# A recurrent attention kernel, forward and backward: steps in three head parts, division after the weighted sum, output projections split by output columns

## The chip, the cores and the metric

The kernel runs on one core of one Trainium2 chip. The metric is the device time of one execution in microseconds (us). The profile used here is one execution taken by the hardware profiler. Its engines are PE (matrix multiplications), PEld (the loading of a matmul's stationary operand, the "weights", which may overlap PE), DVE, ACT and POOL (elementwise engines) and SP (which issues the DMA transfers). "Granted clock" is the share of PE's full clock that the profile says was granted.

## The reference

The reference computes a block with layer norm, a dense MLP with squared ReLU, and a recurrent attention, and then all gradients. Cut to what matters (S = 2048 rows, D = 512, 32 heads of 128, segments of 32 rows, 8 memory rows):

```python
mem = mem0
for s in range(64):
    xs = x[:, s*32:(s+1)*32, :]
    h = concatenate([mem, xs], axis=1)            # 8 + 32 = 40 rows
    q, k, v = h @ Wq, h @ Wk, h @ Wv              # per head
    p = softmax(where(mask, q @ k.T * scale, -1e9))
    o = (p @ v) @ Wo                              # sum over heads and their 128 columns
    mem = o[:, :8, :]                             # the next segment's memory
    outs.append(o[:, 8:, :])
out = x + concat(outs) + mlp(layernorm(x))        # xs are rows of layernorm(x)
# then jax.vjp(out): gradients of x, mem0, Wq, Wk, Wv, Wo, w1, b1, w2, b2
```

The memory makes both directions serial: 64 forward steps, then 64 backward steps in reverse order, each needing the result of the one before.

## The kernel before

The program has seven stretches: MLP and weight transposes; projections of the rows that no later step needs (the first 8 rows of each segment, the "left rows"); the forward recurrence; the left rows' attention; the backward recurrence; the left rows' gradients; and the weight gradients. The 32 heads are spread as 4 groups (g) of 8 (k). A step's 32 rows take 32 of the array's 128 columns, so four matmuls, one a group, stand side by side as column tiles (`tile_position=(0, 32 * g)`).

A projection over all heads is summed. Each of the four column tiles holds the partial sum of its own group; a matmul with a selection matrix adds the four:

```python
# forward, after the weighted sum:
def wo_half(R, OT, B):
    for k in range(B * KK, (B + 1) * KK):
        for g in range(HG):
            nc.tensor.matmul(R[32 * g:32 * g + 32, :], lhsT=OT[:, k, g, :], rhs=Wo[:, g * KH + k, :],
                             start=(k == 0), stop=(k == KH - 1), tile_position=(0, 32 * g))
# backward, three such sums (t = v, k, q) of 8 * 4 matmuls 512 columns wide:
def back_proj(gTs):
    R = pbig("ps_gR")
    ...
            nc.tensor.matmul(R[32 * g:32 * g + 32, :], lhsT=gX[:, k, g], rhs=WT[t][:, g * KH + k, :], ...)
    Rs = bs.tile([P, D], F32, name="bRs", tag="bRs")
    nc.any.tensor_copy(Rs[:], R[:])
# ... and the sum over groups, which gives the next step's input:
    for dc in range(DC):
        nc.tensor.matmul(psm[:, dc * M:(dc + 1) * M], lhsT=Rs[:, dc * P:(dc + 1) * P], rhs=sel[:],
                         start=True, stop=True)
```

At the end of each backward step, three gradient tiles are turned and written out, through a staging tile with two buffers:

```python
def spill_nat(gX, t, r0):
    gN = bs.tile([P, GW], BF16, name="gNat", tag="gNat")        # pool bs: two buffers
    for B in range(2):
        ps = trp.tile([P, 1024], BF16, name="ps_nat", tag="tr")
        for k in range(KK):
            transpose_to(ps[:, k * P:(k + 1) * P], gX[:, B * KK + k])
        nc.any.tensor_copy(gN[:, B * 512:(B + 1) * 512], ps[:, 0:512])
    dma(S_G[r0:r0 + 32, t, :].rearrange("r (g c) -> g r c", g=HG), gN[:])   # 256 KB, shape [4][32][1024]
```

The left rows' gradients and the sums over groups for the output rows come after the recurrence, block by block, for 16 blocks (`left_done`, `finish_back`, which calls `sum_rows` over four stored partial sums).

## Time and profile before

| | us |
|---|---|
| median of 4 runs | 5743.66 (5728.2 to 5751.35) |
| MLP, weight transposes | 712 |
| left-row projections | 152 |
| forward recurrence, 64 steps | 1321 |
| left-row attention, 16 blocks | 666 |
| backward recurrence, 64 steps | 1698 |
| left-row gradients, 16 blocks | 344 |
| weight gradients, with a gap | 852 |

The same kernel by stretches. The columns are the stretch, its length, the busy us and instructions of PE, PEld, DVE, ACT and POOL, then the granted clock, the DMA engines' share and GB/s. The five stretches shown are the forward recurrence, the left rows' attention, the backward recurrence, the left rows' gradients, and the gap in the weight gradients:

```profile
864.00:2185.00 1321.00, 1086.75 (x17016) 525.44 (x17008) 406.54 (x1155) 526.35 (x1022) 66.44 (x186) 0.83 0.33 107
2185.00:2851.00 666.00, 318.15 (x6046) 196.21 (x6046) 214.79 (x624) 223.22 (x704) 154.73 (x144) 0.59 0.52 169
2851.00:4549.00 1698.00, 1164.14 (x20900) 662.96 (x20904) 455.52 (x2045) 503.14 (x1277) 17.27 (x66) 0.75 0.38 111
4549.00:4893.00 344.00, 163.38 (x2009) 73.38 (x2000) 32.65 (x74) 39.05 (x67) 50.79 (x43) 0.71 0.40 125
...
5326.00:5602.00 276.00, 2.60 (x13) 1.06 (x12) 17.14 (x36) 0.58 (x1) 66.39 (x57) 0.51 0.24 73
```

In the last one PE did 2.6 us of work in 276: it waited for the chain of group sums.

One backward step in the chain of work that ended last (start us, us, what; the short pieces left out):

```profile
3508.60 7.58 PE ps_gR L677 x95
3516.20 0.59 ACT bRs L681
3516.84 1.07 PE ps_bm L894 x8
3518.22 0.40 PE ps_nat L201 x4
3518.64 0.43 DVE gNat L691
3519.13 7.75 DMA S_G<-gNat
3527.01 0.44 DVE gNat L691
...
3535.29 7.88 PE ps_gR L677 x94
```

A backward step of 26.5 us is thus about 7.8 us of waiting for a store (the third gNat needs the buffer of the first, whose 256 KB must have landed), about 8 us of flips, scores and outer products, about 8 us of the 512-wide sum `ps_gR`, and 1.7 us of group sum. The waits of that stretch say the same (waiter, what it waited for: us in total, times, longest):

```profile
DVE gNat L691 <- DMA S_G<-gNat: 420.8, 63, 6.9
...
PE ps_tr L201 <- DVE gNat L691: 322.5, 63, 5.4
```

### The profile page before, as it was taken

Reading aid. Unit: us, or ns where it says so; the run is one execution under the profiler, and the core shown is the slowest. Engines: PE = TensorE matmul, PEld = TensorE weight load, DVE = VectorE, ACT = ScalarE, POOL = GpSimd, SP = SyncE. Lnnn points to the kernel's source line nnn. Section 1 sums busy time; section 2 is a strip of 40 time slices with the busy share of each in tenths; the row PEclk is TensorE's granted clock in tenths of the full one; section 3 lists DMA queues with packets and bytes.
Section 4 is the critical chain, followed back from the end, with each engine's and each line's share of the span. In section 5 each row is a group of like instructions: output and inputs, shape, how many; then the busy total and the mean of one; then the engine's idle time right before and its main releaser. Section 6 shows DMA issues by size and latency. Waiting matters only on the chain.

```text
span 5745.4 us, 121908 instructions
## 1 busy us (share of the span) xinstructions
PE 3770.1 (66%) x52292; PEld 1932.4 (34%) x52292; DVE 1368.9 (24%) x4348; ACT 1525.5 (27%) x3440; POOL 440.7 (8%) x619
## 2 busy tenths in 40 slices
PE   3923588888888884555376666767667644899009
PEld 2511233343443432333233333333333322344004
DVE  5610023333333332333222222222222201000000
ACT  1300033444444442333222323222232211011001
POOL 0000000000000001222200000000000011111220
PEclk8966898888888886565577777777777777899559
DMA  5296553333333325455543433333333334666222
GB/s 167 111 210 185 192 204 105 105 104 107 107 104 107 105 96 202 158 155 168 172 118 107 118 108 112 113 111 114 107 113 111 91 119 138 221 211 227 87 59 103
DMA packets 517090, 768.84 MB, mean 134 GB/s; under 512 B 152882, under 2 KB 230339, under 8 KB 513987
## 3 DMA queue, kind: packets, MB, share of 16 engines
q1 hardware_dynamic: 516546, 761.04, 42.4%
q8 instruction: 409, 6.70, 0.5%
q14 instruction: 135, 1.10, 0.1%
HBM read 401.22 MB, written 343.42 MB: 130 GB/s over the span
## 4 chain that ended last, share of the span: by engine, by line
PE 49%; DMA 25%; DVE 11%; ACT 7%; SPq 4%; issue 3%; POOL 2%; DVEq 0%; POOLq 0%; ACTq 0%
PE ps_gR L677 9%; DMA S_G<-gNat 9%; PE ps_proj L423 7%; PE ps_gw L929 7%; PE ps_tr L201 6%; PE ps_R L524 4%; PE ps_out L666 3%; PE ps_gwo L942 2%; PE ps_m L620 2%; PE ps_wgh L474 1%; DMA gXL<-S_GL 1%; ACT OT L433 1%; DMA S_PART<-part 1%; PE ps_bm L894 1%; DMA S_WT<-wtt 1%
## 5 line engine op out<-in xcount | busy, mean ns | idle before, releaser
L423 PE MATMUL ps_proj<-Wqkv,hT 128*32 128x512 bf16 x6144 | 488.1, 423 | 0.3 <-DVE hT L572 0.3
L691 DVE COPY gNat<-ps_nat 128x512 bf16<-128x512 bf16 x239 | 101.4, 424 | 1422.0 <-PE ps_nat L201 870.1
L201 PE MATMUL ps_tr<-ident,gON 128*128 128x128 bf16 x640 | 88.6, 287 | 327.8 <-DVE gNat L691 322.5
L929 PEld LDWEIGHTS <-HNc 128*128 128x128 bf16 x1920 | 188.2, 98 | 265.2 <-issue 40.0
L691 ACT COPY gNat<-ps_nat 128x512 bf16<-128x512 bf16 x241 | 141.1, 585 | 496.4 <-DMA S_G<-gNat 431.8
L524 PE MATMUL ps_R<-Wo,OT 128*32 128x512 bf16 x2048 | 172.5, 469 | 86.2 <-ACT OT L433 86.2
L677 PE MATMUL ps_gR<-WT_28394,gv 128*32 128x512 bf16 x2048 | 224.0, 615 | 0.0
L942 PE MATMUL ps_gwo<-GOc,on_71965 128*128 128x512 bf16 x160 | 36.5, 392 | 273.4 <-DMA GOc<-S_GO 273.4
L681 ACT COPY bRs<-ps_gR 128x512 f32<-128x512 f32 x80 | 46.8, 585 | 622.3 <-PE ps_gR L677 614.2
L423 PEld LDWEIGHTS <-hT 128*32 128x32 bf16 x6144 | 151.5, 102 | 172.9 <-issue 72.7
L423 PE MATMUL ps_proj<-WoT,goT 128*32 128x512 bf16 x2048 | 159.8, 386 | 39.2 <-POOL goT L841 39.2
L201 PEld LDWEIGHTS <-gON 128*128 128x128 bf16 x640 | 55.1, 121 | 342.4 <-issue 321.1
L677 PE MATMUL ps_gR<-WT_28396,gk 128*32 128x512 bf16 x2048 | 166.5, 483 | 0.0
L666 PE MATMUL ps_out<-gST,b_kN 32*128 32x32 bf16 x2048 | 129.6, 184 | 30.0 <-DVE gkL L877 23.6
L433 DVE COPY vT<-ps_tr 128x512 bf16<-128x512 bf16 x65 | 27.6, 425 | 503.1 <-issue 481.7
L474 PEld LDWEIGHTS <-PT 32*32 32x32 bf16 (+1 forms) x5120 | 94.2, 105 | 147.1 <-DVE PT L465 89.4
L899 POOL COPY goT<-gTblk 128x96 bf16<-128x96 bf16 x63 | 16.8, 267 | 1606.3 <-PE ps_proj L423 1606.3
L382 PE MATMUL ps_w_2850<-ghn,xnN 128*128 128x512 bf16 x16 | 6.2, 389 | 191.7 <-DMA ghn<-S_GH1N 191.7
L620 PE MATMUL ps_m<-sel,Rs 128*128 128x8 f32 x504 | 100.2, 327 | 43.5 <-ACT Rs L613 43.5
L479 ACT CAST ON<-ps_wgh 128x512 bf16<-128x512 f32 x128 | 74.9, 585 | 193.6 <-PE ps_wgh L474 193.6
L666 PE MATMUL ps_out<-gST,b_kLs 8*128 8x32 bf16 x2048 | 124.6, 183 | 0.8
L620 PEld LDWEIGHTS ps_m<-sel,Rs 128*128 128x128 f32 x504 | 94.3, 280 | 84.5 <-ACT Rs L613 84.5
(944 smaller groups left out, 7256.4 us busy)
## 6 DMA issues: line engine op xcount, KB each, us to landing
S_G<-gNat SPq DMA_DIRECT2D x240, 256.0 KB
S_PART<-part SPq DMA_DIRECT2D x128, 256.0 KB
b_part<-S_PART SPq DMA_DIRECT2D x64, 512.0 KB
S_VTA<-vT SPq DMA_DIRECT2D x64, 320.0 KB
b_vT<-S_VTA SPq DMA_DIRECT2D x64, 320.0 KB
S_KA<-kN SPq DMA_DIRECT2D x64, 256.0 KB
S_QA<-qN SPq DMA_DIRECT2D x64, 256.0 KB
S_VA<-vN SPq DMA_DIRECT2D x64, 256.0 KB
```

Of the source, the lines that this page charges most:

```text
L201: nc.tensor.transpose(ps_ap, in_ap, ident[base:base + k, base:base + k])
L423: nc.tensor.matmul(ps[32 * g:32 * g + 32, :], lhsT=hT[:, dc, :], rhs=W[:, dc, c:c + 512], start=(dc == 0), stop=(dc == DC - 1), tile_posit ...
L433: nc.any.tensor_copy(dst, ps[:, 0:KK * P].rearrange("p (k g r) -> p k g r", k=KK, g=HG))
L474: nc.tensor.matmul(ps[32 * g:32 * g + 32, k * P:(k + 1) * P], lhsT=PT[32 * g:32 * g + n, k, i, :], rhs=V[32 * g:32 * g + n, (B * KK + k) * ...
L479: nc.any.tensor_copy(dst[:, B * 512:(B + 1) * 512], ps[:])
L524: nc.tensor.matmul(R[32 * g:32 * g + 32, :], lhsT=OT[:, k, g, :], rhs=Wo[:, g * KH + k, :], start=(k == 0), stop=(k == KH - 1), tile_posit ...
L620: nc.tensor.matmul(psm[:, dc * M:(dc + 1) * M], lhsT=Rs[:, dc * P:(dc + 1) * P], rhs=sel[:], start=True, stop=True)
L666: nc.tensor.matmul(p3[:, k, :], lhsT=N_[32 * g:32 * g + m, k * P:(k + 1) * P], rhs=X(k)[32 * g:32 * g + m], start=(i == 0), stop=(i == len ...
L677: nc.tensor.matmul(R[32 * g:32 * g + 32, :], lhsT=gX[:, k, g], rhs=WT[t][:, g * KH + k, :], start=(i == 0), stop=(i == 3 * KH - 1), tile_p ...
L691: nc.any.tensor_copy(gN[:, B * 512:(B + 1) * 512], ps[:, 0:512])
L929: nc.tensor.matmul(ps[:], lhsT=HNc[:, rc, dc * P:(dc + 1) * P], rhs=gn[:, rc, u * 512:(u + 1) * 512], start=(rc == 0), stop=(rc == RC_ALL ...
L942: nc.tensor.matmul(ps[:], lhsT=on[:, rc, i * P:(i + 1) * P], rhs=GOc[:, rc, :], start=(rc == 0), stop=(rc == RC_ALL - 1))
```

## The change

The intent, stretch by stretch:

- A projection over the heads is split by output columns instead of by groups. Each of the four column tiles now holds 128 of the 512 output columns and sums all groups, so the sum over groups and its float32 matmuls disappear, and the step's result is transposed once.
- Steps work in three parts of 3, 3 and 2 heads a group. In the forward, the division of the softmax moves from the probabilities to the weighted sum.
- Stores of a step, and the work that prepares them, stand in the program behind the next step's chain.
- The left rows' part of the key and value gradients is computed within the backward steps, and their spill within every fourth step. The stretches for the left rows' gradients and group sums go.
- Many scratch arrays are merged (q, k and v into `S_NA`), and the gathered rows for the weight gradients come straight from the small memory arrays.

The core of the diff (cut; the rest renames, merges scratch arrays and rebuilds masks):

```diff
-        def back_proj(gTs):
-            R = pbig("ps_gR")
-            ...
-                        nc.tensor.matmul(R[32 * g:32 * g + 32, :], lhsT=gX[:, k, g], rhs=WT[t][:, g * KH + k, :],
-                                         start=(i == 0), stop=(i == 3 * KH - 1), tile_position=(0, 32 * g))
+        def gather(R, XT, W, ks, first, last):
+            for k in ks:
+                for g in range(HG):
+                    for c in range(DC):
+                        nc.tensor.matmul(R[32 * c:32 * c + 32, 0:P], lhsT=XT[:, k, g, :],
+                                         rhs=W[:, g * KH + k, c * P:(c + 1) * P],
+                                         start=(first and k == ks[0] and g == 0),
+                                         stop=(last and k == ks[-1] and g == HG - 1), tile_position=(0, 32 * c))
 ...
-                psm = btr.tile([P, 512], F32, name="ps_bm", tag="tr")
-                for dc in range(DC):
-                    nc.tensor.matmul(psm[:, dc * M:(dc + 1) * M], lhsT=Rs[:, dc * P:(dc + 1) * P], rhs=sel[:], ...)
+                psm = btr.tile([P, 1024], BF16, name="ps_bm", tag="tr")
+                transpose_to(psm[:, 0:P], Rb[:])
 ...
+            def rest(...):
+                dma(to_rows(S_RB, s * SEG), Rf[:])
+                dma(to_rows(S_MBB[s], 0), Rb[:])
+                spill_nat(((2, gv), (1, gk), (0, gq)), s * SEG, (dve_copy, act_copy))
+                if j == 0:
+                    left_done(b, gkL, gvL)
+                    finish_back(b)
+            later.append(rest)
-        for b in range(NB - 1, -1, -1):
-            left_done(b)
-            finish_back(b)
 ...
             # left rows' attention (pool ls: one buffer, ld: two)
+            NLt = ls.tile([P, 3, GW], BF16, name="l_N", tag="l_N")
+            kvM = ls.tile([P, 2, GW], BF16, name="l_kvM", tag="l_kvM")
+            dma(kvM[:].rearrange("p t c -> p (t c)"),
+                S_NA[b].rearrange("g j r t c -> (g j) r (t c)")[:, 0:M, GW:3 * GW])
```

## The prediction

> **What bounds the kernel now.** No engine does: PE is busy 66%, DVE 24%, ACT 27%, DMA 42% (the page). Cutting the span into stretches at the first and last times of each stage's tiles gives: MLP and weight transposes 712 us; left-row projections 152; forward recurrence 1321 (64 steps, 20.6 each); left-row attention 666; backward recurrence 1698 (26.5 a step); left-row gradients 344; weight gradients 852, of which 276 is PE idle: ps_gwo waits 273 us for GOc (waits view), while the chain walks block by block through the group sums S_RA.
>
> A forward step (timeline) is a dependent chain; its tail from the last projection to the next hT takes about 9.5 us. A backward step has a stall: the third gNat waits about 5.2 us for the store S_G (PE ps_tr <- DVE gNat 322 us, gNat <- S_G), then 8 us of dscores and outers, 8 us of ps_gR, 1.7 us of bRs and ps_bm.
>
> **What the change does, by stretch.**
> - Group sum gone. It removes the f32 ps_m (1.06-1.88 us) and 0.58 us Rs copy, replaced by a 128x128 copy and one transpose: about -1.5 us on the path of each step. PE then issues four times as many R/gR matmuls (128x128 instead of 128x512, still four column tiles). The weighing matmuls of the same width run four in 0.06 us (fast clock) or 0.106 (slow), so 128 cost 1.9-3.4 us against 2.1-3.6: neutral.
> - Forward: three parts overlap better, division leaves the path: I estimate a chain near 15 us. But stores shaped [4][32][...] run on few engines: 2 KB packets go at about 43 per us, 92 ns each, four in flight. The Trainium skill ("DMA: Bandwidth & Descriptors", section on why a DMA increments its semaphore by 16) says k is the largest number up to 16 that divides both slowest dims; here 4, and the trace agrees. Those engines carry about 17 us a step now and about 16 after; N3 has two buffers and its 768 KB store is issued a step late. So 16.8 us a step, 1080 in all (-240).
> - Left-row attention: no partial-sum copies, no 256 KB S_PART stores, no q/k/v flips: 666 to about 370.
> - Backward: 64 more small matmuls (+1.7 us), 256 DVE adds become copies, sum gone. The gNat wait stays (still two buffers for three spills, still ahead of the next flips in the PE order) and may grow, as a 512 KB QK load on the same four engines stands before it: about 27.5 us a step. Left rows now fall into every fourth step with six spills and 384 more matmuls: about 10 more there. 1880 in all, against 1698+344 (-160).
> - Tail: finish_back no longer sums groups and GOc does not wait for it: -275.
> - Left-row projections flip q too: +15.
>
> Sum: 705+165+1080+370+1880+30+570 = 4800 us.
>
> **Prediction: 4800 us, range 4480 to 5120 (8 in 10).** Chances: faster by over 2% 0.96, within 2% 0.03, slower 0.01.
>
> **Right or wrong would show as.** Forward steps 16-18 us, with ACT's first N copy waiting for S_NA; backward steps 26-29 us with gNat still waiting for S_G, every fourth near 37; ps_gR matmuls at 15-27 ns start to start; no idle stretch between ps_gw and ps_gwo; left-row attention about 20 us a block.
>
> **What would make it wrong.** If 128-column matmuls in column tiles do not hide their weight loads, each gather costs 2-4 us more and backward loses 300-600 us. If 4 to 6 KB runs move faster per engine, forward falls to 15 us (-100). If the gNat wait in the backward doubles behind the QK load, +200; if the spill truly hides behind projections, -250. A lower granted clock in the denser loops would add 5%.

## More of the kernel before

The page of the kernel before, cut to the span, the first line of its busy times (busy us, share of the span, instructions) and the queue that fetches instructions (packets, MB, share of 16 engines' span):

```profile
span 5745.4 us, 121908 instructions
...
PE 3770.1 (66%) x52292; PEld 1932.4 (34%) x52292; DVE 1368.9 (24%) x4348; ACT 1525.5 (27%) x3440; POOL 440.7 (8%) x619
...
q8 instruction: 409, 6.70, 0.5%
```

No engine is full.

## The result, and the profile after

| | before | after |
|---|---|---|
| median us (range, runs) | 5743.66 (5728.2 to 5751.35, 4) | 5183.44 (5180.53 to 5188.78, 4) |
| ratio, 95% interval | | 0.9029 [0.9008, 0.9049] |
| MLP, weight transposes | 712 | 705 |
| left-row projections | 152 | 174 |
| forward recurrence | 1321 | 1053 |
| left-row attention | 666 | 507 |
| backward recurrence | 1698 | 2071 |
| between the recurrence and the weight gradients | 344 | 110 |
| weight gradients | 852 | 559 |

A ratio is the mean time of one kernel's runs over that of the other's in the same rounds, so it is not quite the ratio of the medians quoted beside it. Executions over 1.5% slower than the fastest of the same kernel are left out of the means. Stretches are of the profiled runs (5745.4 and 5179.3 us). The end of the backward recurrence is not cut at quite the same mark: its last outer products ended at 4546 us of 4549 before, and at 4524 after, where the cut stands at 4510. So about 15 us of the 110 belong to the recurrence.

The change is 9.7% faster, and slower than the range of the prediction allowed. The page after, the same lines:

```profile
span 5179.3 us, 196279 instructions
...
PE 3590.4 (69%) x89874; PEld 2270.7 (44%) x89874; DVE 1515.1 (29%) x5110; ACT 1225.2 (24%) x3450; POOL 312.3 (6%) x741
...
q8 instruction: 702, 11.50, 0.9%
```

PE's matmuls went from 52,292 to 89,874 at slightly less busy time. The instruction queue went from 409 packets to 702. The stretches that answer to those before (forward, left rows' attention, backward, the rest before the weight gradients, the weight gradients):

```profile
879.00:1932.00 1053.00, 909.75 (x25779) 543.53 (x25783) 495.01 (x1723) 447.77 (x1279) 181.69 (x505) 0.97 0.39 128
1932.00:2439.00 507.00, 201.07 (x7034) 133.82 (x7022) 168.23 (x423) 78.89 (x177) 43.11 (x68) 0.62 0.58 182
2439.00:4510.00 2071.00, 1403.03 (x49563) 1083.63 (x49563) 615.37 (x2527) 443.62 (x1572) 70.34 (x109) 0.75 0.29 87
4510.00:4620.00 110.00, 30.67 (x1062) 25.27 (x1060) 14.01 (x49) 9.00 (x27) 3.56 (x3) 0.59 0.54 142
4620.00:5179.00 559.00, 555.37 (x2560) 251.02 (x2560) 0.00 (x0) 73.73 (x128) 0.00 (x0) 0.99 0.47 170
```

The gap in the weight gradients is gone: PE is busy 555 of 559 us. The forward recurrence gained what was expected. The backward recurrence holds 2.4 times as many PE matmuls as before and takes 2071 us; it now includes the left rows' gradients, but 1698 + 344 = 2042 us did all of that before. The gain of the change there is nil.

The chain through one backward step after (start us, us, what; "issue" is time in which the engine waited for nothing that the profile shows):

```profile
3179.72 8.11 DMA S_G<-gNat
3187.95 0.43 DVE gNat L383
...
3197.32 0.65 PE ps_gR L485 x35
3197.98 1.17 issue
3199.14 3.46 PE ps_gR L485 x65
3202.60 0.29 issue
3202.89 0.51 PE ps_gR L485 x21
...
3205.59 0.24 PE ps_bm L179
...
3207.42 10.64 DMA S_G<-gNat
```

Two things are to be seen. The store is still on the chain, with 8.11 and then 10.64 us. And between matmuls of one sum, which wait for no other engine, PE stands still for more than a microsecond. The waits of the backward stretch after:

```profile
DVE gNat L383 <- DMA S_G<-gNat: 689.5, 105, 10.7
...
PE ps_tr L179 <- DVE gNat L383: 310.1, 48, 8.3
...
PE ps_gR L485 <- issue: 77.1, 85, 2.5
...
PE ps_gkq L509 <- issue: 51.4, 45, 3.5
PE ps_gRL L485 <- issue: 46.0, 32, 2.0
```

The kernel before had no PE matmul waiting for issue in its backward stretch. In the left rows' attention (waits of that stretch, after):

```profile
PE ps_wgh L470 <- DMA l_kvM<-S_NA: 164.1, 15, 12.7
```

Of 16 blocks, 15 wait about 11 us for a tile with a single buffer.

The trace also records when each 16,384-byte packet of the instruction queue started. A block of 256 instructions is 16,384 bytes: the page's 89,874 matmuls and as many weight loads, 179,748 instructions, fill 702 blocks, and the page counts 702 packets. Between the first and the last backward step the time from one packet's start to the next was:

```
            packets   smallest   1%     5%     median (us)
before          159     4.48     4.76   5.57   10.28
after           382     3.29     3.34   3.39    4.00
```

In the kernel after, a block never came sooner than 3.29 us after the one before, and hardly ever (1%) under 3.34. The Trainium skill ("Runtime: NRT & Kernel Launch", section "Instruction fetch mechanics") describes this queue: the engine's instruction memory is filled by its own DMA queue in blocks of 16 KiB, 256 instructions, and it says that the fetch is mostly hidden because instructions are dispatched more slowly than they are fetched. The first half agrees with the trace (702 packets of 16,384 bytes). The second half is what the experiments below test.

### The profile page after: what moved, and what is told of

Read it like the earlier page. It is cut to its first block, busy times and chain, and to the rows that moved or that the text cites. A ratio compares the mean times of both kernels' runs of the same rounds, so it can differ in the third digit from the quotient of the medians.

```text
span 5179.3 us, 196279 instructions
## 1 busy us (share of the span) xinstructions
PE 3590.4 (69%) x89874; PEld 2270.7 (44%) x89874; DVE 1515.1 (29%) x5110; ACT 1225.2 (24%) x3450; POOL 312.3 (6%) x741
## 4 chain that ended last, share of the span: by engine, by line
PE 53%; DMA 28%; DVE 6%; ACT 5%; issue 4%; SPq 3%; POOL 1%; DVEq 0%; POOLq 0%; ACTq 0%
DMA S_G<-gNat 13%; PE ps_gR L485 11%; PE ps_proj L402 9%; PE ps_gw L953 8%; PE ps_tr L179 5%; PE ps_R L485 4%; PE ps_gwo L966 3%; PE ps_gkq L509 2%; DMA l_kvM<-S_NA 2%; PE ps_wgh L470 2%; DVE ON L475 1%; DMA S_WT<-wtt 1%; ACT OT L380 1%; PE ps_nat L179 1%; PE ps_sc L426 1%
## 5 line engine op out<-in xcount | busy, mean ns | idle before, releaser
L402 PE MATMUL ps_proj<-Wqkv,hT 128*32 128x384 bf16 x9216 | 474.4, 312 | 0.5 <-ACT hT L634 0.3
L485 PE MATMUL ps_gR<-WT_39551,gk 128*32 128x128 bf16 x8192 | 239.1, 275 | 125.2 <-DVE gk L383 66.1
L485 PE MATMUL ps_gR<-WT_39549,gv 128*32 128x128 bf16 x8192 | 243.9, 293 | 6.2 <-issue 5.2
L485 PEld LDWEIGHTS <-gk 128*32 128x32 bf16 x8192 | 178.2, 122 | 157.3 <-DVE gk L383 68.5
L402 PE MATMUL ps_proj<-WoT,goT 128*32 128x384 bf16 (+1 forms) x3072 | 205.7, 352 | 23.3 <-POOL goT L799 23.0
L485 PE MATMUL ps_gR<-WT_48287,gq 128*32 128x128 bf16 x8192 | 197.9, 262 | 24.9 <-issue 24.1
L485 PEld LDWEIGHTS <-gv 128*32 128x32 bf16 x8192 | 201.3, 132 | 25.1 <-ACT gv L859 13.6
L485 PE MATMUL ps_R<-Wo,OT 128*32 128x128 bf16 x8192 | 153.9, 231 | 58.7 <-ACT OT L380 55.6
L485 PEld LDWEIGHTS <-gq 128*32 128x32 bf16 x8192 | 172.9, 121 | 35.5 <-issue 34.3
L485 PEld LDWEIGHTS <-OT 128*32 128x32 bf16 x8192 | 128.3, 103 | 84.0 <-ACT OT L380 78.8
```

Source lines behind the costliest of these rows:

```text
L402: nc.tensor.matmul(ps[32 * g:32 * g + 32, 0:nk * P], lhsT=hT[:, dc, :], rhs=W[:, dc, c:c + nk * P], start=(dc == 0), stop=(dc == DC - 1), ...
L485: nc.tensor.matmul(R[32 * c:32 * c + 32, 0:P], lhsT=XT[:, k, g, :], rhs=W[:, g * KH + k, c * P:(c + 1) * P], start=(first and k == ks[0] a ...
```

## The experiments

The theory for the backward: two separate waits. (S) The supply of instructions: at about 3.4 us for 256, a step of 1378 PE instructions (5.4 blocks) needs 18 us of fetching, and a fourth step, with the left rows, 2160 instructions (8.4 blocks) and 29 us; before, a step had 656. (G) The store of gNat, still with two buffers, on four DMA engines (in the trace just four packets were in flight for 6.3 of the 8.11 us of the first store shown above). Rivals: (W) narrow matmuls lose time in the array or in loading weights, which the prediction named as its first danger; and for the forward, (F) four DMA engines set the step, as the prediction had it. The expectations use other letters: theory F of b_narrow and b_wide is S here, theory S of b_gnat5 and theory E of b_split are G, and theory D of f_split and all2 is F.

All edits are against the kernel after, which was timed in the first batch alone, so differences to it cross batches and chips. The kernel before ran in every batch, with medians of 5733 to 5750 us; differences of some 20 us therefore mean nothing. "Step" is the median time between successive backward steps: ordinary ones, then every fourth.

### 1. Cut each backward sum matmul in two of 64 columns (b_narrow)

```diff
-                    for c in range(DC):
-                        nc.tensor.matmul(R[32 * c:32 * c + 32, 0:P], lhsT=XT[:, k, g, :],
-                                         rhs=W[:, g * KH + k, c * P:(c + 1) * P], ...
+                    for h in range(0, P, wd):                      # wd = 64 in the backward recurrence
+                        for c in range(DC):
+                            nc.tensor.matmul(R[32 * c:32 * c + 32, h:h + wd], lhsT=XT[:, k, g, :],
+                                             rhs=W[:, g * KH + k, c * P + h:c * P + h + wd], ...
```

> Each ps_gR matmul of the backward recurrence is cut into two of 64 columns: same columns, same stored weights, 384 more matmuls and weight loads a step (768 instructions, three blocks of 256). Theory F (PE waits for its instructions: the trace shows one 16 KB instruction block per 3.4 us at the fastest, and PE idle ends at block boundaries): a step grows by 4 to 10 us, the total to 5440 to 5830 us, with more idle put down to issue. Theory A (the array's column time sets the gather's length): no change, under 5235 us.

Measured: 5731.37 us (5710.68 to 5733.98), ratio to the kernel before 0.9995 [0.9955, 1.0034]. The same columns through the array, 768 more PE instructions a step, and the whole gain of the change is gone. The waits of PE, whole run:

```profile
PE ps_gR L486 <- issue: 533.9, 343, 3.5
PE ps_gkq L511 <- issue: 108.8, 63, 2.4
```

The time lies where S expected it (5440 to 5830 us). This agrees with S in place and size, but twice as many matmuls also load twice as many weights, so it doesn't exclude W. Experiment 3 does.

### 2. Undo the split in the backward alone (b_wide)

```diff
+        def wide(R, XT, W, ks, first, last):
+            for k in ks:
+                for g in range(HG):
+                    nc.tensor.matmul(R[32 * g:32 * g + 32, :], lhsT=XT[:, k, g, :], rhs=W[:, g * KH + k, :],
+                                     start=(first and k == ks[0]), stop=(last and k == ks[-1]),
+                                     tile_position=(0, 32 * g))
...
-            gather(R, gv, WT[2], range(KH), True, False)
+            wide(R, gv, WT[2], range(KH), True, False)
...
+            Rw = bs.tile([P, D], BF16, name="bRw", tag="bRw")
+            nc.scalar.copy(Rw[:], R[:])
+            for dc in range(DC):                                  # the group sum is back, in bf16
+                nc.tensor.matmul(psm[:, 32 * dc:32 * dc + 32], lhsT=Rw[:, dc * P:(dc + 1) * P], rhs=sel[:], ...)
```

> The split by output columns undone in the backward part alone: 512-column matmuls, one group per column tile, groups summed by a bf16 matmul with sel. 288 fewer matmuls a step (576 instructions, 2.25 blocks), but about 0.5 to 0.8 us of group sum back on the path. Theory F: 2 to 4 us a step less net, total 4930 to 5080 us, and the issue idle of about 175 us on ps_gR, ps_gkq and ps_gRL nearly gone. Theory A: 5180 to 5250 us.

Measured: 4928.81 us (4906.05 to 4935.36), ratio 0.8595 [0.8558, 0.8632]: 255 us faster than the kernel after, though it brings back the group sum that the change removed. That is 1 us below the range that S gave. (The left rows' sum `ps_gRL` is widened in the same way, and two small stores change their shape with it.) Its instruction packets fell from 702 to 524. The steps went from 29.6 and 44.0 to 25.4 and 41.0 us, and the waits for issue on `ps_gR`, `ps_gkq` and `ps_gRL` are gone from the list. In the backward the split by columns costs more than the sum it saves. The waits for issue that went were 174.5 us; the other 80 us saved are not assigned to a cause (the granted clock of the stretch also rose, from 0.75 to 0.80).

### 3. Add a matmul of one weight column and one moving column beside each (b_tiny)

```diff
                     for c in range(DC):
                         nc.tensor.matmul(R[32 * c:32 * c + 32, 0:P], lhsT=XT[:, k, g, :], ...
+                        if extra:
+                            nc.tensor.matmul(R[32 * c:32 * c + 1, P:P + 1], lhsT=XT[:, k, g, 0:1],
+                                             rhs=W[:, g * KH + k, c * P:c * P + 1], ...
```

> Beside each of the 384 gather matmuls of a backward step stands one more with a single weight column and a single moving column, into an unused column of the same bank: 768 more PE instructions a step, like the run that cut each gather matmul in two, but with almost no array or weight-load work. Theory S (a step is paced by the supply of instruction blocks, 256 instructions in 3.4 us): three more blocks a step, about 8 to 10 us, so a backward step near 41 us and some 5720 us in all, as in the run with 64-column halves (41.3 us, 5731 us). Rival W (narrow matmuls lose time on the array or on loading 32 weight columns): a load and a matmul of one column cost little, 384 pairs at most 2 to 3 us, so a step of 34 to 36 us and 5250 to 5400 us in all. In the waits, S expects PE ps_gR <- issue of about 500 us, W less than 200.

Measured: 5767.21 us (5763.91 to 5768.47). One output, the gradient of the first memory, came out wrong (relative error 0.18); the added column is read by nothing, and the control flow doesn't depend on values, so the time stands. Six of the seven runs of the kernel before in this batch (5737.45 to 5752.49 us) were marked slow, because the seventh, at 5643.43 us, lay over 1.5% below them; so there is no ratio here, and the run is compared with experiment 1.

The extra matmuls are nearly empty, and an ordinary step took 37.9 to 40.3 us and a fourth one 51.1, against 37.2 to 39.5 and 50.5 when the matmuls were cut in two. The same number of instructions gave nearly the same time, whether they carried half the columns or one. The waits of the sums, whole run (L490 is the extra matmul), lie near the 500 us that S expected; W expected under 200:

```profile
PE ps_gR L485 <- issue: 223.4, 167, 3.1
PE ps_gR L490 <- issue: 220.7, 173, 2.3
```

Part of the chain through one step of it:

```profile
3402.54 1.36 issue
3403.90 0.17 PE ps_gR L490
3405.13 0.39 PE ps_gkq L515 x23
3405.51 1.86 issue
3407.37 1.13 PE ps_gkq L515 x62
...
3409.75 1.37 issue
3411.11 0.17 PE ps_gR L490
3413.43 1.43 issue
3414.86 0.17 PE ps_gR L490
3417.17 1.16 issue
3418.33 0.17 PE ps_gR L490
```

PE resumes at 3403.90, 3407.37, 3411.11, 3414.86 and 3418.33: every 3.47 to 3.75 us. Between the pauses it runs freely: by the table below, a block of 256 takes 1.45 to 2.16 us from the end of one pause to the start of the next, 11 to 17 ns for a load with its matmul, so this isn't a fixed price of a matmul. Counting PE's instructions from the start, and setting the fetches beside them (worked out from the trace's records):

```
fetch starts   PE stops .. resumes    instructions so far / 256
3401.59        3402.37 .. 3403.90     497.62
3404.95        3405.35 .. 3407.37     498.62
3408.43        3409.53 .. 3411.11     499.62
3412.24        3413.21 .. 3414.86     500.62
3415.99        3416.95 .. 3418.33     501.62
```

Every pause stands at the same place within a block of 256, and ends 2.3 to 2.7 us after a fetch began. In the kernel after, the pauses of the step shown above stand at 429.75 and 430.75, and in the step after it at 434.75, 435.75 and 436.75. Counted so over the whole backward stretch, every pause of a matmul for issue longer than 0.5 us stands at one place, give or take one instruction: 133 of 133 at instructions 193 to 195 of a block in the kernel after, 421 of 421 at 193 to 195 in b_narrow, 412 of 412 at 159 to 161 in b_tiny; they end 2.2 to 3.4 us after a fetch began. W has no reason for such places. This is as near to a direct view of S as the trace gives.

The waits don't make up the whole growth. From the first to the last step mark the kernel after took 2036 us, b_narrow 2563 and b_tiny 2600; PE's waits for issue in the backward stretch grew by 505 and 400 us. The granted clock of the stretch also fell, from 0.75 to 0.61 in both. What part it has in the rest was not tested.

### 4. Five buffers for gNat (b_gnat5)

```diff
-                gN = wk.tile([P, GW], BF16, name="gNat", tag="gNat")
+                gN = gp.tile([P, GW], BF16, name="gNat", tag="gNat")     # a pool of its own, five buffers
```

> Five gNat buffers in place of two (backward). Theory S (the third spill's wait for the first store S_G, in front of the next flips in PE's order, is on the path): normal steps lose about 4 to 5 us, the fourth ones about 10, total 4750 to 4900 us. Rival E (the four DMA engines that carry S_G and QK are the limit): the wait moves to another transfer and the total falls by less than 100 us.

Measured: 4798.94 us (4794.71 to 4800.11), ratio 0.8374 [0.8344, 0.8404]: 384 us faster than the kernel after, for one number. The total is in the expected range; the steps fell to 22.9 to 23.5 and 39.3 us, the ordinary ones by more than the 4 to 5 us expected and the fourth by less than the 10. The wait of the flips for gNat is gone; that for issue stayed (the backward stretch):

```profile
PE ps_gR L485 <- issue: 87.2, 98, 2.2
...
PE ps_gkq L509 <- issue: 72.9, 47, 3.2
```

So G and S are separate waits, and G is the larger.

### 5. The S_G store in four pieces (b_split)

```diff
-                dma(S_G[r0:r0 + 32, t, :].rearrange("r (g c) -> g r c", g=HG), gN[:])
+                for g in range(HG):
+                    dma(S_G[r0:r0 + 32, t, g * GW:(g + 1) * GW], gN[32 * g:32 * g + 32, :])
```

> Each S_G store issued as four stores of 32 partitions, so that 16 DMA engines carry it and not 4. Theory E (engines): S_G lands in 4 to 5 us after its issue, not 8 to 10, steps fall by 3 to 4 us, total 4930 to 5000 us. If the wait is latency and issue order instead: total above 5110 us.

Measured: 4854.52 us (4845.28 to 4856.93), ratio 0.847 [0.8432, 0.8507]: 329 us faster than the kernel after, with the same bytes, the same buffers and four times as many issues. That is 75 us below the expected range: the gain was underrated. On the chain that ended last, a piece of the S_G store had a median of 4.0 us, against 8.9 in the kernel after. The wait of `ps_tr` for gNat fell from 310 to 116 us. The Trainium skill ("DMA: Bandwidth & Descriptors", section "Why a DMA increments its semaphore by 16 and not by 1") says that a transfer is dealt to at most 16 engines, by the largest number up to 16 that divides the slowest dimensions of both sides. For a shape of [4][32][1024] that is 4, for [32][1024] it is 16. This run agrees with it in its effect: same bytes, a wait little over a third as long.

### 6. The two backward fixes together (b_ws)

The edit is 2 and 5 together.

> The 512-wide gather with its group sum in the backward, and S_G stored in four pieces over 16 engines; nothing else. Alone the two saved 255 and 329 us (4929 and 4855 against 5183). Theory: they take away different waits of the same step, instruction supply and the store, so most of the sum survives: 4620 to 4700 us, a backward step near 24.5 to 25.5. Rival (both only shorten the same stall ahead of the next flips, whichever is later): barely under the better of the two, 4800 to 4850, a step of 27 or more.

Measured: 4742.23 us (4737.95 to 4745.45), against the kernel after 441 us faster. No ratio, for the reason given in 3. Alone the two saved 255 and 329, together 584; three quarters of the sum survived. Both expectations missed: the two gains don't simply add. Its steps were 23.7 to 24.7 and 31.2 us, and the wait for issue in the sums is gone, while DVE still waited 196 us for the store.

### 7. Two buffers in the left rows' attention (l_dbuf)

```diff
-            NLt = ls.tile([P, 3, GW], BF16, name="l_N", tag="l_N")
-            dma(NLt[:], S_NL[b])
+            NLt = ld.tile([P, 2, GW], BF16, name="l_N", tag="l_N")
+            dma(NLt[:], S_NL[b][:, 1:3, :])                          # q was loaded and not used
-            kvM = ls.tile([P, 2, GW], BF16, name="l_kvM", tag="l_kvM")
+            kvM = ld.tile([P, 2, GW], BF16, name="l_kvM", tag="l_kvM")
-            acc = ld.tile([P, D], F32, name="l_acc", tag="l_acc")
+            acc = ls.tile([P, D], F32, name="l_acc", tag="l_acc")        # to make room
```

> Left-row attention: l_N (its unused q part not loaded) and l_kvM in two buffers instead of one, paid for with one buffer of l_acc. Theory W (ps_wgh waits about 10 us of a 28 us block for l_kvM, because its one buffer comes free only when the last outer products are done, and the loads start then): the stretch of about 520 us falls by 100 to 150, total 5030 to 5085 us. Rival B (bandwidth: the loads of a block need that time anyway): under 50 us gained, total above 5130 us.

Measured: 5025.97 us (5012.78 to 5030.27), ratio 0.8758 [0.874, 0.8775]: 157 us faster than the kernel after and 4 below the expected range. From the last forward step to the first backward step it took 387 us instead of 522, and the wait of `ps_wgh` for l_kvM is gone.

### 8. The forward's stores over 16 engines (f_split)

```diff
-                dma(S_NA[b, :, j], N3[:])
+                for g in range(HG):
+                    dma(S_NA[b, g, j], N3[32 * g:32 * g + 32])
-                dma(to_rows(S_O, s * SEG), ON[:])
+                for g in range(HG):
+                    dma(S_O[s * SEG:(s + 1) * SEG, g * GW:(g + 1) * GW], ON[32 * g:32 * g + 32, :])
```

> S_NA and S_O of the forward recurrence issued as four stores of 32 partitions each, so over 16 DMA engines. Theory D (the prediction: the four engines set the forward step): step from 16.5 to about 15 us, total 5080 to 5100 us. Rival P (PE and its dependent chain set it, the N3 buffer is never waited for): within 25 us of 5183.

Measured: 5172.09 us (5165.94 to 5184.82), ratio 0.9023 [0.9006, 0.904], a forward step of 16.58 us against 16.48. Four engines did not set the forward step. In the profile after, nothing waits for the store of N3; PE is busy 910 of 1053 us at a granted clock of 0.97.

### 9 and 10. A version that beats both (all1, all2)

all1 takes together the wide backward sum (2), three gNat buffers (all that fits beside it), S_G in four pieces (5), the load of q and k in four pieces as well, and two buffers in the left rows' attention (7). all2 adds the forward's split stores (8).

```diff
+            for g in range(HG):
+                dma(QK[32 * g:32 * g + 32].rearrange("p t c -> p (t c)"),
+                    S_NA[b, g, j].rearrange("r t c -> r (t c)")[:, 0:2 * GW])
```

> b_wide, three gNat buffers, S_G and QK over 16 engines, and l_dbuf together. If the three causes add (255 us fewer instructions, about 380 us store wait, about 120 us left-row loads): 4380 to 4480 us, backward steps 23 to 24 us with no gNat wait and no issue idle. If taking away one wait only uncovers another: above 4600 us.

> all1 with the forward stores split too. Theory D: 90 us under all1. Rival P: within 30 us of all1.

Measured: all1 4425.11 us (4418.12 to 4431.26), ratio 0.7717 [0.7703, 0.7731]; all2 4430.39 us (4427.36 to 4435.61), ratio 0.7727 [0.7716, 0.7739], so the forward's split is worth nothing here either. all1 is 23% faster than the kernel before and 15% faster than the kernel after. Both lie in their expected ranges. In all1 no matmul of the backward waits for issue, but DVE still waited 42 us for the S_G store. Its left rows' attention and its backward recurrence:

```profile
1900.00:2279.00 379.00, 219.43 (x7362) 144.55 (x7362) 173.77 (x450) 85.87 (x196) 45.24 (x73) 0.69 0.75 240
2279.00:3778.00 1499.00, 1257.14 (x27687) 683.10 (x27687) 659.52 (x2575) 471.96 (x1589) 108.53 (x172) 0.92 0.43 119
```

PE is now busy 84% of the backward, and the granted clock went from 0.75 to 0.92. An ordinary step takes 18.8 us, a fourth one 37.9. The remaining price is in the fourth.

| run | us | ordinary step, fourth step, us | PE instruction packets |
|---|---|---|---|
| before | 5743.66 | 25.5 to 27.1 (no fourth kind) | 409 |
| after | 5183.44 | 28.8 to 29.9, 44.0 | 702 |
| b_narrow | 5731.37 | 37.2 to 39.5, 50.5 | 894 |
| b_tiny | 5767.21 | 37.9 to 40.3, 51.1 | 894 |
| b_wide | 4928.81 | 24.4 to 25.8, 41.0 | 524 |
| b_gnat5 | 4798.94 | 22.9 to 23.5, 39.3 | 702 |
| b_split | 4854.52 | 25.2 to 25.6, 34.9 | 702 |
| b_ws | 4742.23 | 23.7 to 24.7, 31.2 | 524 |
| all1 | 4425.11 | 18.8, 37.9 | 524 |

## Why the prediction was wrong

The direction was right, and the sum was 379 us short. By stretch, predicted and measured: 705 and 705 for the start; 165 and 174 for the left rows' projections; 1080 and 1053 for the forward; 370 and 507 for the left rows' attention; 1880 and 2071 for the backward; 30 and 110 for the tail; 570 and 559 for the weight gradients. Three terms were mis-sized: backward (+191), left rows' attention (+137) and tail (+80).

**Backward, "128 cost 1.9-3.4 us against 2.1-3.6: neutral" and "64 more small matmuls (+1.7 us)".** This is the step that failed. It compared array time, from matmuls elsewhere in the trace that came in short bursts, and array time was indeed near: the page's groups for `ps_gR` give 681 us busy against 512, in which pauses are partly counted. What it left out is that each matmul must also be fetched. Four times as many matmuls made the sums of a step 768 instructions, three blocks of 3.4 us, where they had been 192. Issue waits of `ps_gR`, `ps_gkq` and `ps_gRL` come to 174.5 us in the backward stretch; taking the narrow sums away (b_wide) saved 255. The prediction came near it: "if 128-column matmuls in column tiles do not hide their weight loads, each gather costs 2-4 us more and backward loses 300-600 us". The size was above the 191 us lost, and the cause was another: b_tiny shows an added matmul with one weight column costing as much as one with 32. As to the sizes: it said 27.5 us for an ordinary step and about 10 more for a fourth; measured means were 29.4 and 42.7, 13.3 more.

**"ps_gR matmuls at 15-27 ns start to start"** was given as the sign of success. Pauses apart they do run at that pace (a mean of 21 ns in the kernel after, gaps over 0.15 us left out); but 256 instructions in 3.4 us are 27 ns for a weight load with its matmul, so a long row of them averages no better than the upper end.

**Backward, "the gNat wait stays ... and may grow".** Right. The wait of the flips was 310 us, against 322, with larger single waits (8.3 us at most, against 5.4). What the prediction missed is that this was the largest thing to be had: more buffers alone were worth 384 us, and a store over 16 engines 329. It was carried into the sum as a fixed price.

**Left rows' attention, "666 to about 370".** The work was costed, 20 us a block, and not the load that each block needs. l_kvM has one buffer, so its load can't start before the last use in the block before, and 15 of 16 blocks wait 11 us: 164 us, more than the whole miss of 137. With two buffers the stretch measured 387 (522 by the same marks before), so the costing of the work was good.

**Tail, 30.** It took 110 us. The chain through it holds 18 us of the last step's own work (the stretch is cut inside that step), 31 us of four gNat stores, one after the other with nothing left to hide them, then the last block's rows, and 36 us of loads for the weight gradients (GOc 12, gn 24). The prediction took the group sums out of this stretch and left 30 us for all that stays. In all1, with the stores in four pieces, 82 us still passed from the last transposed result to the weight gradients. This was read from the trace and not tested alone.

**Forward, "16.8 us a step, 1080 in all".** The number was right (16.5 us, 1053) and the reason wrong, so that it came out was luck. It had four DMA engines set the step and ACT wait for the store of N3. No such wait exists, and spreading the store changed nothing (f_split). The step is a chain of PE work, at a granted clock of 0.97, against 0.83 before. That the store is issued "a step late" holds for the order of the program and not for the execution: in the trace it was issued after the last write of N3 in the same step, with a median of 1.1 us between.

**Weight gradients and the gap, -275.** Right: 559 us, PE busy 555, no wait for the gathered rows.

**Stays open.** Why blocks of instructions start no closer than 3.2 us when one packet takes 1.1; why a fourth step of all1 still costs 19 us more than the others; what part of the rise in granted clock (0.82 after, 0.90 in all1), and of its fall in b_narrow and b_tiny, is cause and what is effect; and why the gradient of the first memory was wrong in b_tiny.

## What to carry to other kernels

Count instructions as well as array time before cutting a matmul into narrower ones: on PE of this chip 256 instructions took no less than 3.2 us to supply in any of these runs, and mostly 3.4 or more, so a row of weight loads and matmuls that could run faster than 25 to 27 ns a pair will stand still in lumps, which the profile shows as waits for "issue" inside one accumulation. Before costing a rearrangement, price the waits that it leaves in place: here five staging buffers instead of two, or a store shaped so that it spreads over 16 engines, were each worth more than half of what the whole change gave. When a loop is made shorter, look again at each tile with one buffer, because its load now has less to hide behind.

## What the Trainium skill lacked or had wrong

- "Runtime: NRT & Kernel Launch", section "Instruction fetch mechanics", says that instruction fetch is hidden, since dispatch is slower than the fill. It isn't on PE for narrow matmuls: waits for issue of 174.5 us in the backward stretch of the kernel after and of 642.7 us (533.9 + 108.8) in b_narrow, whose pauses over 0.5 us in the backward all stand at one place in a block of 256 instructions. No page gives the rate; these runs show successive blocks starting no sooner than 3.21 us apart (b_split), with a median of 3.77 in the backward of b_narrow, the densest, while one packet itself takes 1.1 us.
- "TensorE: Matmul & The Clock Gate", section "Back-to-back issue gap", gives a floor of about 25 ns per matmul for small moving sizes. With four column tiles side by side, b_tiny ran below it between its pauses: 11 to 17 ns a pair of load and matmul. What held its long rows was the block: 3.47 to 3.75 us for 256 instructions, 27 to 29 ns a pair.
- "DMA: Bandwidth & Descriptors", section "Why a DMA increments its semaphore by 16 and not by 1", has the rule for the number of engines, and the page's advice says what shape to choose. It has no time for what the narrow shape costs in a kernel: cutting one 256 KB store of shape [4][32][1024] into four of [32][1024] saved 329 us of 5183 where the next step waited for it (b_split), and nothing clear of noise where none did (f_split, 11 us).
